# Convolution taps moved off VectorE in the first block, and the last block's last round done in two halves, in a float32 convolution and feed-forward kernel

## Chip, cores and metric

One core of one Trainium2 chip. The metric is the device time of one execution in microseconds; each run also has a profiled span, which begins and ends with the core's first and last recorded instruction and is about 1.8 us shorter. Spans are given to 0.1 us, so a difference with one is good to about 0.05 us. Ratios are the mean time of one kernel's fast runs over that of the other's of the same rounds, so not quite the ratio of the medians that I quote.

## The reference

```python
# x (8, 4096, 192), weight (8, 7), w_in (192, 2048), w_out (2048, 192)
w = softmax(weight)                          # 7 taps for each of 8 heads
c = causal 7-tap convolution of x along the sequence, taps by head
h = c.reshape(32768, 192) @ w_in
g = h * clip(h + 3, 0, 6) / 6
out = g @ w_out                              # float32
```

Of the kernel before, what the change touches and what calls it, by code (L numbers as in the profile page):

```python
# [8 lines left out]
ALU = mybir.AluOpType  # L9
# [7 lines left out]
def kernel(  # L17
# [21 lines left out]
    nc = tc.nc  # L39
# [3 lines left out]
    H, KC = weight.shape  # L43
# [3 lines left out]
    N = 512  # L47
# [107 lines left out]
    class Rounding:  # L155
# [10 lines left out]
        def load(self):  # L166
            self.st = self.load_words()
# [105 lines left out]
    def swap(part):  # L273

        to = slice(OTHER + part.start, OTHER + part.stop)
        nc.sync.dma_start(out=y[D2:P, to], in_=y[0:D2, part])  # L276
        nc.sync.dma_start(out=y[0:D2, to], in_=y[D2:P, part])
# [19 lines left out]
    def take():  # L297
        return free_banks.pop(0)

    def give(b):  # L300
        free_banks.append(b)
# [128 lines left out]
    def dff_half(k):  # L430
        return g[:, :, k // G, k % G]

    def mm(bank, j, x, w, q, ps_, first, last):

        cols = slice(q * QS, (q + 1) * QS)
        return [
            lambda p=p: nc.tensor.matmul(  # L437
                out=bank[j * QS : (j + 1) * QS], lhsT=w_out[:, p, w, cols], rhs=x[:, p],
                start=(first and p == ps_[0]), stop=(last and p == ps_[-1]),
                tile_position=(0, j * QS),  # L440
            )
            for p in ps_
        ]
# [5 lines left out]

    every = range(NP)  # L450

    def store_rows(i, k, q, xt, j, dma=nc.sync):

        t0 = i * TB + k * N
        dma.dma_start(
            out=out[t0 : t0 + N, q * QS : (q + 1) * QS].rearrange("(t r) d -> r t d", r=QS),
            in_=xt[j * QS : (j + 1) * QS].rearrange("r (t d) -> r t d", d=QS),
        )

    def out_direct(i, work):  # L460
# [41 lines left out]
        5: (None, T1), 6: (S2, T2), 7: (S3, T3),  # L502
    }

    def product(bank, j, n, q, ks=every):
        x, w = prod[n]
        return mm(bank, j, S1 if n == 5 else x, w, q, ks, True, True)

    def four(*parts):

# [5 lines left out]
    def three(n, n4, q4):  # L516
        return four(*[(n, q) for q in range(NQ)], (n4, q4))
# [11 lines left out]
    def rows(q):  # L529
        return slice(q * QS, (q + 1) * QS)  # L530
# [9 lines left out]
    def add(out, x, y, op=ALU.add):  # L540
        nc.vector.tensor_tensor(out=out, in0=x, in1=y, op=op)  # L541

    def store(i, c, k, half_, qs=range(NQ), queues=(nc.sync,)):

        xt = ot.tile([P, N], F32, name="xt")
        r = slice(qs[0] * QS, (qs[-1] + 1) * QS)
        nc.vector.transpose(out=xt[r], in_=c[r])  # L547
        for q in qs:
            store_rows(i, k, half_ * NQ + q, xt, q, queues[q % len(queues)])

    def sums_tiles():
        return (cs.tile([DH, N], F32, name=f"c{k}") for k in range(6))
# [3 lines left out]
    def out_last(i):  # L556

        both = nc.sync, nc.scalar
        p1, p2, p4, p5, u2, u3 = sums_tiles()
        b, bank = three(1, 2, 0)  # L560
        nc.scalar.copy(out=p1[:], in_=bank[m])
        piece(p2, 0, bank, NQ)
        give(b)
        g_sums(nc.vector, (2,), every, 4)
        b, bank = four((2, 1), (2, 2), (4, 0), (4, 1))
        for dst, q, j in ((p2, 1, 0), (p2, 2, 1), (p4, 0, 2), (p4, 1, 3)):
            piece(dst, q, bank, j)
        give(b)
        g_sums(nc.vector, (4,), every, 4)
        add(p2[:], p1[:], p2[:])  # L570
        store(i, p2, 0, 0)
        b7, bank7 = three(7, 5, 0)
        piece(p5, 0, bank7, NQ)
        b, bank = three(6, 5, 1)
        piece(p5, 1, bank, NQ)
        add(u2[:], p1[:], bank[m])
        give(b)
        add(u3[:], u2[:], bank7[m])
        give(b7)
        two = slice(0, 2 * QS)  # L580
        add(p4[two], u3[two], p4[two], ALU.subtract)
        store(i, p4, 1, 0, range(2))
        b, bank = by_quarters(5, 2)
        pieces(p5, 2, bank)
        give(b)
        add(u2[:], u2[:], p5[:])
        add(p5[:], u3[:], p5[:])
        store(i, p5, 1, 1)
        b, bank = three(3, 4, 2)
        add(u2[:], u2[:], bank[m])  # L590
        store(i, u2, 0, 1, queues=both)
        add(u3[rows(2)], u3[rows(2)], bank[rows(NQ)], ALU.subtract)
        store(i, u3, 1, 0, range(2, 3), queues=both[::-1])
        give(b)

    def out_strassen(i, conv):
        p1, p2, p4, p5, u2, u3 = sums_tiles()
# [55 lines left out]
    with tc.manual_schedule():  # L653
        nc.vector.tensor_reduce(out=sm[:], in_=e_sb[:], axis=AX.X, op=ALU.add)
        nc.vector.tensor_scalar_add(sm[:], sm[:], 1e-9)
        nc.vector.reciprocal(sm[:], sm[:])
        nc.vector.tensor_tensor(
            out=c_sb[:], in0=e_sb[:], in1=sm[:].to_broadcast([P, KC]), op=ALU.mult
        )

        thirds = [slice(s, s + 1) for s in range(K3)]
        pe_third = K3 - 1
        b = take()
        for _ in range(3):

            nc.tensor.matmul(
                out=psum[:, b], lhsT=zeros[:, 0:P], rhs=zeros[:], start=True, stop=True
            )
        for k in range(KC):
            nc.scalar.mul(diag[:, k], ident[:], c_sb[:, k : k + 1])  # L670
            nc.tensor.matmul(
                out=psum[:, b], lhsT=diag[:, k], rhs=x_tiles[0][:, pe_third, k : k + N],
                start=(k == 0), stop=(k == KC - 1),
            )
        conv0 = conv_units(0, thirds[:pe_third], 2)
        per = len(conv0) // pe_third
        for k, u in enumerate(conv0):
            if k == 5:
                split(0)
                clamp(0)  # L680
            elif k == per - 3:
                join(0, more=False)
            elif k == per:
                nc.scalar.copy(out=y[:, pe_third], in_=psum[:, b])
                give(b)
                swap(thirds[0])
                swap(thirds[pe_third])
                load(AHEAD)
                split(1)
                clamp(1)  # L690
            elif k == per + 6:
                split(2)
                join(1)
                clamp(2)
            u()
        swap(thirds[1])
        split(3)
        split(4)
        join(2)
        clamp(3)  # L700


        parts = [(c, group) for p in range(0, NP, 2) for group in (OWN, OTHER)
                 for c in (p, p + 1)]
        early = [(c, group, (take(), take())) for c, group in parts[:4]]
        order = (0, pe_third, 1)
        for c in range(2):
            for slot, group, bs in early:
                if slot == c:
                    for s in order[:2]:  # L710
                        h_mm(c, group, bs, s, order)
        for c, group, bs in early:
            h_mm(c, group, bs, order[2], order)

        slots = [0, 1, 2, 3, 5, 6, 8, 10, 12, 14]
        n = 3
        for slot, (c, group) in enumerate(parts):
            first = slot < len(early)
            if first:
                bs = early[slot][2]  # L720
            else:
                bs = take(), take()
                for s in range(K3):
                    h_mm(c, group, bs, s)
            more = slot in slots

            def between():
                if more:
                    join(n)
                    clamp(n + 1)  # L730

            if slot == 6:
                x_tiles[1] = load_x(1)
            h_out(c, group, bs, (lambda: None) if first else between)
            if more:
                split(n + 2)
                if first:
                    between()
                n += 1
        while n < len(units):  # L740
            join(n)
            clamp(n + 1)
            split(n + 2)
            n += 1
        w_sums()
        start_pools.close()
        ss = ctx.enter_context(tc.tile_pool(name="ss", bufs=1))
        p5s = ctx.enter_context(tc.tile_pool(name="p5s", bufs=3))
        cs = ctx.enter_context(tc.tile_pool(name="cs", bufs=1))
        ot = ctx.enter_context(tc.tile_pool(name="ot", bufs=4))  # L750

        def conv_and_swap(i):
            return conv_units(i, [slice(0, K3)]) + [lambda: swap(slice(0, K3)), y_sums]

        out_direct(0, conv_and_swap(1))
        x_tiles[2] = load_x(2)

        S1 = ss.tile([P, NP, N], F32, name="s1")[:]
        left = []
        for i in range(1, NB):  # L760
            h_phase(left)
            if i + 1 < NB:
                left = out_strassen(i, conv_units(i + 1, [slice(0, K3)]))
            else:
                out_last(i)
            if i + 2 < NB:
                x_tiles[i + 2] = load_x(i + 2)
# [33 lines left out]
```

## The kernel before: what the change touches

The kernel works through 32 blocks of 1024 tokens. The channels are in three thirds of 64; the tile `y` holds, for each third, 512 tokens in the lower and the other 512 in the upper 64 partitions ("own"). A swap by DMA gives each half the other's tokens ("other"). Both orders are multiplied with the 8 pairs of `w_in` units; a relu (ScalarE) and a gate (VectorE) turn each bank (the piece of TensorE's result memory, PSUM, that takes one product) into `g`; then `g` is multiplied with `w_out`. From block 1 on this is a Strassen scheme. The weights arrive as float64 words, and each of 16 units is rounded to float32 by `split` (VectorE), `clamp` (ScalarE) and `join` (VectorE, then a GpSimd product); `AHEAD` units are loaded in advance. A *pair* is, from here on, a pair of banks: 16 of them, counted from 0, make the first block's first projection (the multiplication with `w_in`), 12 matmul instructions each. In the code cuts `...` stands for what is left out.

The start, with VectorE making thirds 0 and 1 in halves of 256 tokens and TensorE making third 2 through diagonal matrices:

```python
        for k in range(KC):
            nc.scalar.mul(diag[:, k], ident[:], c_sb[:, k : k + 1])
            nc.tensor.matmul(out=psum[:, b], lhsT=diag[:, k], rhs=x_tiles[0][:, pe_third, k : k + N], ...)
        ...
        conv0 = conv_units(0, thirds[:pe_third], 2)      # 14 half taps for third 0, 14 for third 1
        for k, u in enumerate(conv0):
            if k == 5:         split(0); clamp(0)
            elif k == per - 3: join(0, more=False)
            elif k == per:
                nc.scalar.copy(out=y[:, pe_third], in_=psum[:, b]); give(b)
                swap(thirds[0]); swap(thirds[pe_third]); load(AHEAD)
                split(1); clamp(1)
            elif k == per + 6: split(2); join(1); clamp(2)
            u()
        swap(thirds[1])
        split(3); split(4); join(2); clamp(3)
        ...                                              # four pairs of banks are begun in thirds 0, 2, then third 1
        slots = [0, 1, 2, 3, 5, 6, 8, 10, 12, 14]        # bank pairs at which a unit is joined
```

The end of the last block:

```python
        b, bank = three(3, 4, 2)                         # the last 32 matmuls, 512 tokens wide
        add(u2[:], u2[:], bank[m])
        store(i, u2, 0, 1, queues=both)                  # transpose, then one DMA for 32 rows
        add(u3[rows(2)], u3[rows(2)], bank[rows(NQ)], ALU.subtract)
        store(i, u3, 1, 0, range(2, 3), queues=both[::-1])
```

## Time and profile before

| | before |
|---|---|
| time, median of 6 runs | 2410.84 us (2410.76 to 2410.96) |
| span | 2409.1 us |
| TensorE busy | 2399.2 us |
| first product (matmul with w_out) on the chain | 58.87 us |
| start of the last product phase | 2366.65 us |
| end of the last transpose | 2405.79 us |

TensorE is nearly the whole span. The *first product* is where the chain that ended last goes over from the first projection to the first multiplication with `w_out`; whatever the start wins must be won there. The *tail* is the time from the start of the last product phase to the end of the span, 42.45 us before. The four VectorE operations behind the last matmul (columns: start us, length us, engine, line, operation, operands, count, idle time before and what ended it):

```profile
2402.91 0.68 DVE L541 TENSOR_TENSOR c<-c,psum 96x512 f32<-96x512 f32 x1 [0.77 <-PE psum L437]
2403.63 0.71 DVE L547 STREAM_TRANSPOSE xt<-c 96x512 f32<-96x512 f32 x1
2404.37 0.69 DVE L541 TENSOR_TENSOR c<-c,psum 32x512 f32<-32x512 f32 x1
2405.09 0.70 DVE L547 STREAM_TRANSPOSE xt<-c 32x512 f32<-32x512 f32 x1
```

VectorE idles 0.77 us until the whole round is multiplied, then works 2.9 us; that idle time is what the change of the last round aims at.

### The profile page before, as it was taken

The page shows a single profiled execution, that of the slowest core. Times are in us where ns is not written, and L with a number is a line of the kernel's source. Part 1 is how long each engine was busy: PE and PEld are TensorE (multiplying, and loading weights), DVE is VectorE, ACT ScalarE, POOL GpSimd, SP SyncE. Part 2 cuts the span into 40 slices and gives each one's busy share as a digit, 9 for nine tenths or more (in the row PEclk, how much of TensorE's full clock was granted, in tenths as well). Part 3 has the DMA queues.
Part 4 walks back from the last instruction along what each step waited for, and adds up shares of the span by engine and source line. Part 5 has one row for each costly group of instructions (what it writes and reads, how often), then busy time and mean ns, then how long its engine had stood idle before and what let it go on. Part 6 is the DMA issues. An engine that isn't in the chain of part 4 may idle for free.

```text
span 2409.1 us, 40076 instructions
## 1 busy us (share of the span) xinstructions
PE 2399.2 (100%) x16468; PEld 1008.8 (42%) x16468; DVE 2088.8 (87%) x2534; ACT 1077.1 (45%) x1827; POOL 671.3 (28%) x280
## 2 busy tenths in 40 slices
PE   9999999999999999999999999999999999999998
PEld 4334444334444344443444434444334444344443
DVE  8788888988888888898888898888898888888896
ACT  7234553345543355433454334553335543355433
POOL 2423321233221333122332223322233312333122
PEclk9999999999999999999999999999999999999999
DMA  5211122101122011221112211122201122111210
GB/s 145 40 26 29 27 40 40 39 18 26 39 41 40 19 35 27 40 41 22 32 27 40 41 34 21 27 40 40 40 18 34 30 40 40 21 34 27 40 27 14
DMA packets 227336, 84.65 MB, mean 35 GB/s; under 512 B 205456, under 2 KB 210576, under 8 KB 227152
## 3 DMA queue, kind: packets, MB, share of 16 engines
q1 hardware_dynamic: 225848, 81.56, 17.1%
q8 instruction: 129, 2.11, 0.4%
q10 hardware_dynamic: 1208, 0.27, 0.1%
q14 instruction: 55, 0.45, 0.1%
q0 software_dynamic: 96, 0.26, 0.0%
HBM read 31.72 MB, written 25.17 MB: 24 GB/s over the span
## 4 chain that ended last, share of the span: by engine, by line
PE 99%; DVE 1%; DMA 0%; issue 0%; ACTq 0%; SPq 0%; DVEq 0%
PE psum L311 50%; PE psum L437 48%; DVE y L263 0%; DMA x<-in_x_dram 0%; DMA y<-y 0%; DVE c L541 0%; ACTq L92 0%; DVE scale L174 0%; DVE y L259 0%; DVE sig L199 0%; DVE scale L195 0%; DVE top L178 0%; DVE xt L547 0%; SPq L276 0%; DVEq L259 0%
## 5 line engine op out<-in xcount | busy, mean ns | idle before, releaser
L437 PE MATMUL psum<-g,w_out 128*32 128x512 f32 x9312 | 1163.6, 592 | 0.0
L311 PE MATMUL psum<-y,w_in 64*128 64x512 f32 x3664 | 885.1, 592 | 2.1 <-DVE y L263 1.9
L497 POOL TENSOR_TENSOR s<-g 128x1024 f32<-128x1024 f32 x124 | 293.5, 2367 | 1645.1 <-DVE g L321 1645.1
L317 ACT ACTIVATE r<-psum,half 128x512 f32<-128x512 f32 x1024 | 641.3, 688 | 241.3 <-PE psum L311 234.2
L437 PEld LDWEIGHTS psum<-g,w_out 128*32 128x32 f32 x9312 | 337.4, 110 | 811.7 <-issue 769.9
L321 DVE SCALAR_TENSOR_TENSOR g<-r,psum 128x512 f32<-128x512 f32 x1024 | 641.8, 681 | 4.8 <-ACT r L317 1.1
L437 PE MATMUL psum<-s,w_out 128*32 128x512 f32 x1488 | 638.5, 592 | 0.0
L311 PEld LDWEIGHTS psum<-y,w_in 64*128 64x128 f32 x3664 | 430.2, 187 | 378.7 <-issue 299.4
L311 PE MATMUL psum<-y,w_in_t 64*128 64x512 f32 x1984 | 523.8, 592 | 0.0
L403 DVE TENSOR_TENSOR psum<-psum,p 128x512 f32<-128x512 f32 x496 | 324.6, 694 | 196.0 <-PE psum L311 187.3
L263 DVE SCALAR_TENSOR_TENSOR y<-x,c_sb,y 128x1536 f32<-128x1536 f32 (+1 forms) x210 | 416.6, 1991 | 6.6
L533 ACT COPY c<-psum 32x512 f32<-32x512 f32 x188 | 108.7, 578 | 600.7 <-PE psum L437 599.9
L497 POOL TENSOR_TENSOR g<-g 128x1024 f32<-128x1024 f32 x124 | 338.0, 2725 | 9.7
L311 PEld LDWEIGHTS psum<-y,w_in_t 64*128 64x128 f32 x1984 | 247.1, 186 | 194.3 <-issue 124.9
L541 DVE TENSOR_TENSOR c<-c,psum 32x512 f32<-32x512 f32 (+1 forms) x187 | 128.1, 685 | 81.8 <-ACT c L533 75.8
L396 ACT COPY psum<-psum 128x512 f32<-128x512 f32 x248 | 138.9, 571 | 72.6 <-PE psum L311 57.4
L437 PEld LDWEIGHTS psum<-s,w_out 128*32 128x32 f32 x1488 | 162.4, 110 | 1.2 <-issue 1.2
L399 ACT COPY p<-psum 128x512 f32<-128x512 f32 x248 | 133.2, 591 | 40.7 <-PE psum L311 40.0
L497 DVE TENSOR_TENSOR g<-s,g 128x2048 f32<-128x2048 f32 x62 | 139.3, 2287 | 3.9 <-POOL g L497 2.3
L497 DVE TENSOR_TENSOR g<-g 128x2048 f32<-128x2048 f32 x62 | 139.4, 2289 | 2.0 <-PE psum L437 1.0
L601 ACT COPY c<-psum 96x512 f32<-96x512 f32 x30 | 17.4, 581 | 174.5 <-PE psum L437 174.5
L606 ACT COPY c<-psum 96x512 f32<-96x512 f32 x30 | 17.4, 581 | 170.0 <-PE psum L437 170.0
(46 smaller groups left out, 431.9 us busy)
## 6 DMA issues: line engine op xcount, KB each, us to landing
out_dram<-xt SPq DMA_DIRECT2D x382, 64.0 KB, 2.0
y<-y SPq DMA_DIRECT2D x62, 384.0 KB, 4.8
x<-in_x_dram SPq DMA_DIRECT2D x55, 388.5 KB, 5.7
stage<-in_moe_w_in_dram SPq DMA_DIRECT2D x16, 192.0 KB, 4.4
stage<-in_moe_w_out_dram SPq DMA_DIRECT2D x8, 384.0 KB, 5.2
x<-in_x_dram SPq DMA_DIRECT2D x7, 384.0 KB
y<-y SPq DMA_DIRECT2D x6, 128.0 KB, 2.3
x<-in_x_dram SPq DMA_DIRECT2D x2, 128.0 KB, 4.4
```

The lines of the kernel that those rows point to most:

```text
L263: nc.vector.scalar_tensor_tensor(out=to, in0=x[:, part, k + t : k + t + W], scalar=c, in1=to, op0=ALU.mult, op1=ALU.add,)
L311: nc.tensor.matmul(out=psum[:, b], lhsT=w[r], rhs=y[r, third_of_y], start=start, stop=stop, skip_group_check=onto,)
L317: nc.scalar.activation(r6, h, ACT.Relu, bias=half[:], scale=1.0 / 6.0)
L321: nc.vector.scalar_tensor_tensor(out=out, in0=r6, scalar=1.0, in1=h, op0=ALU.min, op1=ALU.mult)
L396: nc.scalar.copy(out=psum[:, bank["b"]], in_=psum[:, bank["a"]])
L399: nc.scalar.copy(out=self.p5[:], in_=psum[:, bank["e"]])
L403: nc.vector.tensor_tensor(out=psum[:, to], in0=psum[:, bank["b"]], in1=self.p5[:], op=ALU.add)
L437: lambda p=p: nc.tensor.matmul(out=bank[j * QS : (j + 1) * QS], lhsT=w_out[:, p, w, cols], rhs=x[:, p], start=(first and p == ps_[0]), sto ...
L497: engine.tensor_tensor(out=o[:, r], in0=a[:, r], in1=b[:, r], op=op)
L533: nc.scalar.copy(out=dst[rows(q)], in_=src[rows(j)])
L541: nc.vector.tensor_tensor(out=out, in0=x, in1=y, op=op)
L601: nc.scalar.copy(out=p1[:], in_=bank[m])
```

## The change

The intent at the start: take work off VectorE (tap 0 of third 1 to ScalarE, taps 5 and 6 to TensorE), exchange TensorE's own third 2 as soon as it is copied, and spread the joins so that the first pairs are less crowded. Some lines only change place: split 3, and with it clamp 3, now comes behind join 2. At the end: do the last round in two halves of 256 tokens, so that VectorE begins while TensorE still multiplies.

```diff
+        pe_taps = KC - 2
+        def pe_tap(b, part, k, first): nc.tensor.matmul(...)     # one tap through a diagonal matrix
         for k in range(KC):
             nc.scalar.mul(diag[:, k], ident[:], c_sb[:, k : k + 1])
+            pe_tap(b, pe_third, k, 0)
+        nc.scalar.mul(y[:, 1], x0[:, 1, 0:N], c_sb[:, 0:1])      # tap 0 of third 1
+        b1 = take()
+        pe_tap(b1, 1, pe_taps, pe_taps)                          # tap 5
+        order = (pe_third, 0, 1)
...
-        for k, u in enumerate(conv0):
+        for k, u in enumerate(conv0[: per + 2 * pe_taps]):
             elif k == per - 3:
                 join(0, more=False)
+                split(1)
                 nc.scalar.copy(out=y[:, pe_third], in_=psum[:, b])
                 swap(thirds[pe_third])
                 clamp(1)
             elif k in (per, per + 1):
+                if k == per:
+                    swap(thirds[0]); load(AHEAD)
+                    begin(0, OWN)                                # first pair, thirds 2 and 0
+                    pe_tap(b1, 1, pe_taps + 1, pe_taps)          # tap 6
+                continue
+            elif k == per + 4: join(1); split(2); clamp(2)
+        add(y[:, 1], psum[:, b1], y[:, 1]); give(b1)
         swap(thirds[1])
-        split(3); split(4); join(2); clamp(3)
+        join(2); split(3); clamp(3); split(4)
...
-        slots = [0, 1, 2, 3, 5, 6, 8, 10, 12, 14]
+        slots = [0, 1, 3, 4, 6, 7, 9, 10, 12, 13]
... (last round of the last block)
+        for t in range(0, N, N // 2):
+            b = take(); bank = psum[:, b]; ts = slice(t, t + N // 2)
+            side_by_side(...)                                    # the same products, tokens ts
+            add(u2[:, ts], u2[:, ts], bank[m, ts])
+            store(i, u2, 0, 1, queues=both, tokens=ts)
+            add(u3[rows(2), ts], u3[rows(2), ts], bank[rows(NQ), ts], ALU.subtract)
+            store(i, u3, 1, 0, range(2, 3), queues=both[::-1], tokens=ts)
+            give(b)
```

More of the change, by code (lines that the diff above doesn't have):

```diff
@@ L431, in dff_half, with mm @@
         return g[:, :, k // G, k % G]
-    def mm(bank, j, x, w, q, ps_, first, last):
+    def mm(bank, j, x, w, q, ps_, first, last, tokens=slice(0, N)):
         cols = slice(q * QS, (q + 1) * QS)
@@ L437, in mm @@
             lambda p=p: nc.tensor.matmul(
-                out=bank[j * QS : (j + 1) * QS], lhsT=w_out[:, p, w, cols], rhs=x[:, p],
+                out=bank[j * QS : (j + 1) * QS, tokens], lhsT=w_out[:, p, w, cols],
+                rhs=x[:, p, tokens],
                 start=(first and p == ps_[0]), stop=(last and p == ps_[-1]),
@@ L450, with store_rows @@
     every = range(NP)
-    def store_rows(i, k, q, xt, j, dma=nc.sync):
+    def store_rows(i, k, q, xt, j, dma=nc.sync, tokens=slice(0, N)):
         t0 = i * TB + k * N
         dma.dma_start(
-            out=out[t0 : t0 + N, q * QS : (q + 1) * QS].rearrange("(t r) d -> r t d", r=QS),
-            in_=xt[j * QS : (j + 1) * QS].rearrange("r (t d) -> r t d", d=QS),
+            out=out[t0 + tokens.start : t0 + tokens.stop, q * QS : (q + 1) * QS].rearrange("(t r) d -> r t d", r=QS),
+            in_=xt[j * QS : (j + 1) * QS, tokens].rearrange("r (t d) -> r t d", d=QS),
         )
@@ L503, with product @@
     }
-    def product(bank, j, n, q, ks=every):
+    def product(bank, j, n, q, ks=every, **tokens):
         x, w = prod[n]
-        return mm(bank, j, S1 if n == 5 else x, w, q, ks, True, True)
+        return mm(bank, j, S1 if n == 5 else x, w, q, ks, True, True, **tokens)
     def four(*parts):
@@ L541, in add, with store @@
         nc.vector.tensor_tensor(out=out, in0=x, in1=y, op=op)
-    def store(i, c, k, half_, qs=range(NQ), queues=(nc.sync,)):
+    def store(i, c, k, half_, qs=range(NQ), queues=(nc.sync,), tokens=slice(0, N)):
         xt = ot.tile([P, N], F32, name="xt")
         r = slice(qs[0] * QS, (qs[-1] + 1) * QS)
-        nc.vector.transpose(out=xt[r], in_=c[r])
+        nc.vector.transpose(out=xt[r, tokens], in_=c[r, tokens])
         for q in qs:
-            store_rows(i, k, half_ * NQ + q, xt, q, queues[q % len(queues)])
+            store_rows(i, k, half_ * NQ + q, xt, q, queues[q % len(queues)], tokens)
     def sums_tiles():
@@ L588, in out_last @@
         store(i, p5, 1, 1)
-        b, bank = three(3, 4, 2)
-        add(u2[:], u2[:], bank[m])
-        store(i, u2, 0, 1, queues=both)
-        add(u3[rows(2)], u3[rows(2)], bank[rows(NQ)], ALU.subtract)
-        store(i, u3, 1, 0, range(2, 3), queues=both[::-1])
-        give(b)
+        for t in range(0, N, N // 2):
+            b = take()
+            bank = psum[:, b]
+            ts = slice(t, t + N // 2)
+            side_by_side(*[
+                product(bank, j, n, q, tokens=ts)
+                for j, (n, q) in enumerate([(3, 0), (3, 1), (3, 2), (4, 2)])
+            ])
+            add(u2[:, ts], u2[:, ts], bank[m, ts])
[3 more added lines that the diff above has]
+            give(b)
     def out_strassen(i, conv):
@@ L662, with pe_tap @@
         pe_third = K3 - 1
+        pe_taps = KC - 2
+        x0 = x_tiles[0]
+        def pe_tap(b, part, k, first):
+            nc.tensor.matmul(
+                out=psum[:, b], lhsT=diag[:, k], rhs=x0[:, part, k : k + N],
+                start=(k == first), stop=(k == KC - 1),
+            )
         b = take()
@@ L670, with begin @@
             nc.scalar.mul(diag[:, k], ident[:], c_sb[:, k : k + 1])
-            nc.tensor.matmul(
-                out=psum[:, b], lhsT=diag[:, k], rhs=x_tiles[0][:, pe_third, k : k + N],
-                start=(k == 0), stop=(k == KC - 1),
-            )
+            pe_tap(b, pe_third, k, 0)
[3 more added lines that the diff above has]
+        order = (pe_third, 0, 1)
+        parts = [(c, group) for p in range(0, NP, 2) for group in (OWN, OTHER)
+                 for c in (p, p + 1)]
+        early = {}
+        def begin(c, group):
+            early[c, group] = take(), take()
+            for s in order[:2]:
+                h_mm(c, group, early[c, group], s, order)
         conv0 = conv_units(0, thirds[:pe_third], 2)
         per = len(conv0) // pe_third
-        for k, u in enumerate(conv0):
+        for k, u in enumerate(conv0[: per + 2 * pe_taps]):
             if k == 5:
@@ L682 @@
                 join(0, more=False)
-            elif k == per:
+                split(1)
                 nc.scalar.copy(out=y[:, pe_third], in_=psum[:, b])
                 give(b)
-                swap(thirds[0])
                 swap(thirds[pe_third])
-                load(AHEAD)
-                split(1)
                 clamp(1)
-            elif k == per + 6:
+            elif k in (per, per + 1):
+                if k == per:
+                    swap(thirds[0])
+                    load(AHEAD)
+                    begin(0, OWN)
+                    pe_tap(b1, 1, pe_taps + 1, pe_taps)
+                continue
+            elif k == per + 4:
+                join(1)
                 split(2)
-                join(1)
                 clamp(2)
             u()
+        add(y[:, 1], psum[:, b1], y[:, 1])
+        give(b1)
         swap(thirds[1])
+        join(2)
         split(3)
+        clamp(3)
         split(4)
-        join(2)
-        clamp(3)
-        parts = [(c, group) for p in range(0, NP, 2) for group in (OWN, OTHER)
-                 for c in (p, p + 1)]
-        early = [(c, group, (take(), take())) for c, group in parts[:4]]
-        order = (0, pe_third, 1)
-        for c in range(2):
-            for slot, group, bs in early:
-                if slot == c:
-                    for s in order[:2]:
-                        h_mm(c, group, bs, s, order)
-        for c, group, bs in early:
-            h_mm(c, group, bs, order[2], order)
-        slots = [0, 1, 2, 3, 5, 6, 8, 10, 12, 14]
+        for c, group in ((0, OTHER), (1, OWN), (1, OTHER)):
+            begin(c, group)
+        for c, group in parts[: len(early)]:
+            h_mm(c, group, early[c, group], order[2], order)
+        slots = [0, 1, 3, 4, 6, 7, 9, 10, 12, 13]
         n = 3
@@ L719 @@
             if first:
-                bs = early[slot][2]
+                bs = early[c, group]
             else:
```

## The prediction

> **What bounds the kernel now.** I read the page first, then the chain that ended last in order of time, then the timelines of each engine in the first 60 us and the last 15 us, and last the busy time by one-microsecond windows of the start.
>
> The page says that this kernel is a dense TensorE stream with a thin beginning and a thin end:
>
> ```profile
> PE 2399.2 (100%) x16468; PEld 1008.8 (42%) x16468; DVE 2088.8 (87%) x2534; ACT 1077.1 (45%) x1827; POOL 671.3 (28%) x280
> PE 99%; DVE 1%; DMA 0%; issue 0%; ACTq 0%; SPq 0%; DVEq 0%
> ```
>
> So only what is not TensorE on the chain can be won by a change of order. The chain, in order of time, shows both places:
>
> ```profile
> 18.37 3.19 DVE y L263 x7
> ...
> 21.81 0.47 DVE y L263
> 22.28 0.28 DVE scale L174
> 22.57 0.25 SPq L276
> 22.81 0.04 issue
> 22.86 2.40 DMA y<-y
> 25.25 0.04 issue
> 25.30 33.57 PE psum L311 x152
> 58.87 41.34 PE psum L437 x384
> ```
>
> From 6.67 us the chain is VectorE: taps of the convolution and the splits and joins of the first weight units. It makes the last third of y, y goes through the exchange of halves (22.3 to 25.25), and at 25.30 TensorE starts a run that never waits for long again until 2402.9. Everything after 25.30 shifts with it. The end is four VectorE operations and a store after the last matmul: add, transpose, subtract, transpose, from 2402.91 to 2405.79, and the span closes at 2409.1. The part that a reordering can touch is thus the delay before 25.30, about 1 us of waits in the first 35 us after it, and about 6 us of tail: at most some 10 us of 2410.8, and 2% would be 48 us.
>
> VectorE at the start has no gaps worth naming, which is why tap work given to another engine counts (columns: start us, length us, instruction):
>
> ```profile
> 11.30 0.55 DVE L195 SCALAR_TENSOR_TENSOR scale<-stage,scale 128x384 uint32<-128x384 uint32 x1
> 11.77 0.55 DVE L199 SCALAR_TENSOR_TENSOR sig<-top,sig 128x384 f32<-128x384 uint32 x1
> 12.24 2.01 DVE L263 SCALAR_TENSOR_TENSOR y<-x,c_sb,y 128x256 f32<-128x256 f32 x3
> 14.17 0.35 DVE L174 TENSOR_SCALAR scale<-stage 128x384 uint32<-128x384 uint32 x1
> ```
>
> A half tap (128x256) costs 0.395 us start to start (six of them lie between 8.92 and 11.30), a first tap (tensor_scalar) 0.27, a split 0.535 (two starts, 14.17 to 14.71), a join 0.94 (11.30 to 12.24). Three taps from 12.24 to 14.17 should have taken 1.19 us and took 1.93: 0.75 us lost while GpSimd multiplied w_in (12.40 to 13.57). The same happens once more after the second join, at 18.69.
>
> The ScalarE timeline shows what paces the first gates:
>
> ```profile
> 22.59 0.62 ACT L186 ACTIVATE sig<-scale,bias_e 128x384 f32<-128x384 uint32 x1 [3.54 <-DVE scale L174]
> 23.24 0.61 ACT L189 ACTIVATE scale<-sig,bias_e 128x384 uint32<-128x384 f32 x1
> 23.88 0.56 ACT L192 ACTIVATE sig<-stage 128x384 f32<-128x384 uint32 x1
> 24.35 1.25 ACT L317 ACTIVATE r<-psum,half 128x512 f32<-128x512 f32 x2
> ```
>
> The relu of the first pair waits behind the clamp of weight unit 3 (22.59 to 24.35). With a clamp per pair the relus come every 2.90 us (24.35, 27.25, 30.16, 33.07), while TensorE needs 12 instructions x 0.2145 = 2.57 us per pair (a warm start-to-start of 0.43 for two). Banks come free with the gates, some 1.9 us after the relu starts.
>
> **What the Trainium skill says.** SBUF — State Buffer, section "Who interferes with whom": a VectorE instruction with two SBUF inputs, or in a 2-port mode, and a GpSimd instruction that reads SBUF lock each other out. The trace agrees: a tap of 0.47 us took 1.22 at 12.63, beside the GpSimd product. TensorE: Matmul & The Clock Gate, Part 1: an idle TensorE falls to half clock after a window of about 3.4 us. The trace agrees: granted clock 0.50 in 16 to 18 us, after TensorE idled from 12.5 to 14.4. VectorE: DVE Perf Modes, section on the errata: a float32 tensor_tensor takes (N+151)/0.96 ns; 512 columns give 691 and the trace has 684 to 694; so I estimate 424 ns for 256. DMA: Bandwidth & Descriptors, "Anatomy of one DMA": about 2 us fixed, the rest by bytes; a 64 KB store lands here after 2.0 to 2.2 us, so half the bytes should save little.
>
> **The change, step by step.**
>
> 1. VectorE up to y's third 1. Removed: two first-tap halves (0.53 us), now one ScalarE multiply, and four halves of taps 5 and 6 (1.58), now TensorE. Added: one 128x512 addition of the bank (0.65). Net saving 1.46. The two lock collisions stay, since both joins stay ahead. Against it: the ScalarE multiply is queued ahead of clamp 0 and must wait for that third of x (issued 4.27, 5.1 us to land: 9.37), so clamp 0 begins at about 10.1, not 8.77, and join 0 waits some 0.25 us. So third 1 is done near 22.28 - 1.46 + 0.25 = 21.07, and its exchange lands 2.95 us later, near 24.0 instead of 25.25.
>
> 2. TensorE up to there. Its own third (2) is now exchanged as soon as ScalarE has copied it (13.1, landing near 16). Work from the first weight unit (ready near 13.85, because join 0 is later): 40 projection instructions x 0.2145 = 8.58, plus one tap of two instructions at 0.43 = 0.86; the other tap fits before. Split 1 now comes before the last taps of third 0, so that third is ready near 15.05, 0.8 later than before (14.25): TensorE waits there 0.35 us, and perhaps 0.3 for its exchange (15.05 + 2.95 = 18.0). 13.85 + 9.44 + 0.65 = 23.95. TensorE is then just in time for the exchange at 24.0; before, it had about 0.9 us in hand. The idle time before it is short, so I take the clock to stay up.
>
> 3. The first pairs. The 152 instructions start near 24.05 instead of 25.30. But clamp 3 now follows join 2 and split 3: 21.07 + 0.94 + 0.35 gives 22.4, against 22.59, so the first relu is at 24.2, hardly 0.2 earlier. The gates free banks at 26.07, 28.98, 31.88; TensorE could begin pairs 4, 5, 6 at 25.77, 28.64, 31.55: it waits about 0.3 us three times. With joins at pairs 0, 1, 3, 4 the third pair has no clamp, so relu 3 comes at 31.1 instead of 33.07, and from pair 7 there is no wait. Last projection ends near 34.45 + 9 x 2.57 = 57.6; by the same sum the kernel before ends at 58.46, having waited at pairs 7 and 8 only (0.24 and 0.32). Gain of the start: 0.85 us. Later joins have room: weight unit 13, needed about 8.6 us into the second product, was ready at 63.2 of 67.4.
>
> 4. The last round. Matmuls of 256 columns, twice as many: 2 x 16 groups x 0.215 = 6.87 us, as before; the doubled weight loads (0.13 per group of four) hide under 0.215. The first half is ready 3.4 us before the end, but VectorE is busy with the earlier results until 2402.14. Then eight half operations instead of four: additions 0.42, transposes 0.44 (0.71 less 256/0.96 ns), plus 0.03 each: 3.6 us, ending near 2405.75 against 2405.79. What is won is the 0.77 us that VectorE idled; what is paid is four more fixed costs of about 0.17. The last store has 32 KB, not 64: at the 133 GB/s that the last windows show, 0.25 us less. Gain 0.3.
>
> Sum: 2410.8 - 0.85 - 0.3 = 2409.65. I say 2409.6.
>
> **The rivals.** (a) The whole 1.25 us of step 1 arrives at the end, because the relus and clamps overlap better than I count: the chain shows ScalarE nowhere before, which speaks for it; the 2.90 us spacing speaks against. About 2409.2, or 2408.7 if the split also dodges one lock. (b) The wait moves: the ScalarE multiply delays clamp 0 more than I think, or TensorE, now without slack, meets a half clock as in 16 to 18 us, which doubled the time of some 3 us of work. Then start gain is zero or negative: 2410.5 to 2411.2. For it: all three engines are nearly full from 12 to 24. Against: less TensorE idling. (c) The tail: the fourth-last transpose buffer. The split makes seven transposed tiles over four buffers, so the last transpose must wait for the store of three tiles before, issued 2403.06 and landed near 2405.1, just when it is wanted (2405.25). If that store is slow, the tail gains nothing: +0.3. Conversely, if half operations are cheaper, the tail gains up to 0.7.
>
> **Range and chances.** Runs of one kernel differ by under 0.1 us, so the range is my error alone: best cases of (a) and (c) together give 2408.2, (b) with no tail gain 2411. I take 2408.2 to 2410.9. No reading of this profile finds 48 us either way: within 2% is nearly certain.
>
> **What would show it.** Right: third 1's addition ends near 21, the exchange lands near 24, projections end near 57.6, first relu near 24.2 with short waits on gates at pairs 4 to 6; VectorE unbroken from 2401.3 to the last transpose, and a last store of half the bytes. Wrong: clock 0.50 within 15 to 24 us, VectorE waiting for ScalarE at join 0 by over 0.5 us, gates not the thing TensorE waits for, or 256-column matmul groups slower than 0.215 us.

## The result and the profile after

| | before | after |
|---|---|---|
| time, median of 6 | 2410.84 us | 2410.26 us (2409.86 to 2411.30) |
| ratio of the fast runs, 95% interval | 1 | 0.9998 (0.9986 to 1.0011) |
| spans of the 6 runs after | 2409.1 (the profiled run) | 2408.5, 2408.5, 2408.5, 2408.4, 2408.1, 2408.5 |
| first product on the chain | 58.87 us | 58.50 us |
| tail (last product phase to end of span) | 42.45 us | 42.07 us |

The gain is 0.6 us where I said 1.2. The median lies within the predicted range of 2408.2 to 2410.9, but so does the time of the kernel before, so this alone shows little; one of the six runs (2411.30) lies outside of it. The page is unchanged in kind. On the chain the long run of TensorE begins 8 us earlier than before:

```profile
PE 2400.5 (100%) x16536; PEld 1019.8 (42%) x16536; DVE 2089.4 (87%) x2533; ACT 1078.4 (45%) x1828; POOL 672.2 (28%) x280
```

```profile
17.22 41.28 PE psum L311 x184
58.50 41.34 PE psum L437 x384
```

So 184 projection instructions took 41.28 us, while 184 x 0.2145 (the warm pitch) is 39.5. Some 1.8 us of waits are inside by that sum. The timelines of VectorE and ScalarE at the places that the prediction named:

```profile
20.48 0.69 DVE L542 TENSOR_TENSOR y<-psum,y 128x512 f32<-128x512 f32 x1
...
34.56 0.55 DVE L195 SCALAR_TENSOR_TENSOR scale<-stage,scale 128x384 uint32<-128x384 uint32 x1
35.03 1.35 DVE L199 SCALAR_TENSOR_TENSOR sig<-top,sig 128x384 f32<-128x384 uint32 x1
36.31 1.27 DVE L321 SCALAR_TENSOR_TENSOR g<-r,psum 128x512 f32<-128x512 f32 x2
```

```profile
24.18 1.25 ACT L317 ACTIVATE r<-psum,half 128x512 f32<-128x512 f32 x2
```

Third 1 is done at 21.17 (predicted 21.07), the first relu is at 24.18 (24.2). But the second operation of a join took 1.35 us in place of 0.55. GpSimd was at the product of the join before it:

```profile
34.72 1.25 POOL L203 TENSOR_TENSOR w_in<-sig,scale 128x384 f32<-128x384 f32 x1 [3.09 <-DVE sig L199]
```

The joins of pairs 3 and 4 follow each other directly: the first comes behind pair 3's gates, the second ahead of pair 4's gates. The second is held by the first's GpSimd product, and pair 4's gates come late, at 36.31. TensorE's weight loads show who waited:

```profile
37.63 2.44 PEld L311 LDWEIGHTS psum<-y,w_in 64*128 64x128 f32 x13 [0.24 <-DVE g L321]
```

In the tail, VectorE begins at 2401.94 with no idle time, as intended, but stops ahead of its last operation:

```profile
2404.72 0.42 DVE L542 TENSOR_TENSOR c<-c,psum 32x256 f32<-32x256 f32 x1
2405.57 0.44 DVE L548 STREAM_TRANSPOSE xt<-c 32x256 f32<-32x256 f32 x1 [0.43 <-DMA out_dram<-xt]
```

The block's seventh transposed tile waits for a store that still reads its buffer. The chain names the store:

```profile
2403.79 1.68 DMA out_dram<-xt
```

It is the one of the tile two before (transposed at 2403.33), which landed at 2405.47. The last store of the kernel, in both cases one for 32 rows, has half the bytes (first line before, second after; columns: count, size, us from issue to landing):

```profile
out_dram<-xt ACTq DMA_DIRECT2D x1, 64.0 KB, 1.8
out_dram<-xt ACTq DMA_DIRECT2D x1, 32.0 KB, 1.5
```

**Theory, before the experiments.** The start loses what it wins to the first pairs: to the lock between VectorE and GpSimd at the joins of pairs 3 and 4, and to the clamp of unit 3 that now stands behind a join. The tail is shorter by 0.8 us behind the last transpose, which I put down to the smaller last store, and loses 0.4 to the four buffers. **Rivals.** The start brings nothing and the tail all; or the exchange and TensorE's own work, not gates and clamps, set the first projection.

### The profile page after: what moved, and what is told of

The parts are those of the page before. It is cut to its first block, busy times and chain, and to the rows that moved or that the text cites. A ratio compares the mean times of both kernels' runs of the same rounds, so it can differ in the third digit from the quotient of the medians.

```text
span 2408.5 us, 40221 instructions
## 1 busy us (share of the span) xinstructions
PE 2400.5 (100%) x16536; PEld 1019.8 (42%) x16536; DVE 2089.4 (87%) x2533; ACT 1078.4 (45%) x1828; POOL 672.2 (28%) x280
## 4 chain that ended last, share of the span: by engine, by line
PE 99%; DVE 1%; DMA 0%; issue 0%; ACTq 0%; ACT 0%; DVEq 0%
PE psum L311 51%; PE psum L437 48%; DVE c L542 0%; DMA x<-in_x_dram 0%; DVE y L263 0%; DMA out_dram<-xt 0%; DVE xt L548 0%; DVE top L178 0%; ACTq L92 0%; PE psum L676 0%; DVE scale L174 0%; DVE y L259 0%; ACT c L534 0%; DVE scale L195 0%; DVEq L548 0%
## 5 line engine op out<-in xcount | busy, mean ns | idle before, releaser
L437 PE MATMUL psum<-g,w_out 128*32 128x512 f32 (+1 forms) x9376 | 1163.7, 590 | 0.0
L311 PEld LDWEIGHTS psum<-y,w_in 64*128 64x128 f32 x3664 | 437.1, 187 | 369.6 <-issue 290.6
L542 DVE TENSOR_TENSOR c<-c,psum 32x512 f32<-32x512 f32 (+2 forms) x189 | 128.4, 679 | 81.2 <-ACT c L534 75.9
L399 ACT COPY p<-psum 128x512 f32<-128x512 f32 x248 | 133.2, 590 | 40.4 <-PE psum L311 39.5
```

The source lines that it names most:

```text
L311: nc.tensor.matmul(out=psum[:, b], lhsT=w[r], rhs=y[r, third_of_y], start=start, stop=stop, skip_group_check=onto,)
L399: nc.scalar.copy(out=self.p5[:], in_=psum[:, bank["e"]])
L437: lambda p=p: nc.tensor.matmul(out=bank[j * QS : (j + 1) * QS, tokens], lhsT=w_out[:, p, w, cols], rhs=x[:, p, tokens], start=(first and p ...
L542: nc.vector.tensor_tensor(out=out, in0=x, in1=y, op=op)
```

## The experiments

All outputs are right. The kernel before, on three chips, had medians of 2410.92, 2410.89 and 2410.82 us. Every 95% interval of the ratio includes 1 (for e8_best 0.9980 to 1.0005). What is said below of tenths of a microsecond rests on the small scatter and on the one trace that each kernel has.

| run | change against | time, median us (range) | span, median us | first product |
|---|---|---|---|---|
| e1_start_only | after, last round as before | 2410.81 (2410.77 to 2410.91) | 2409.0 | 58.55 |
| e2_tail_only | after, start as before | 2410.53 (2410.48 to 2410.66) | 2408.8 | 59.00 |
| e3_slots_before | after, joins as before | 2410.24 (2410.16 to 2410.61) | 2408.5 | 58.68 |
| e4_slots_apart | after, joins of pairs 3, 4 apart | 2410.07 (2410.04 to 2411.30) | 2408.3 | 58.22 |
| e5_buf5 | after, five buffers | 2409.79 (2409.38 to 2410.10) | 2408.0 | 58.10 |
| e6_clamp_early | after, clamp 3 ahead of join 2 | 2409.72 (2409.65 to 2409.75) | 2408.0 | 57.89 |
| e7_no_taps | after, taps 5, 6 on VectorE | 2411.23 (2410.58 to 2411.32) | 2409.5 | 59.37 |
| e8_best | after, with e4, e5 and e6 | 2409.03 (2408.97 to 2409.09) | 2407.2 | 57.47 |
| e9_three_taps | e8, taps 4, 5, 6 on TensorE | 2408.90 (2408.84 to 2409.76) | 2407.1 | 57.43 |
| e10_own_third_second | after, third 2 exchanged second | 2411.81 (2411.68 to 2413.03) | 2410.0 | 59.91 |

In most of these kernels spans differ less than times do (not in e7, e9 and e10, whose five spans range over 0.7, 0.9 and 1.4 us), so mechanisms are read from spans and traces.

### e1_start_only and e2_tail_only: which part is worth what

The edit of e1 puts back the five lines of the last round; that of e2 puts back the start and the old list of joins.

> The start of the change with the last round of the kernel before. My theory (the start is worth what its trace showed at the first product: its first L437 matmul at 58.50 instead of 58.87 us, so 0.37 us; the tail is worth another 0.2 to 0.4 us of span): span near 2408.7, time 0.3 to 0.4 us under before, and the four last VectorE operations as before (0.70 us each). Rival (the start is worth all of the span's 0.6 us and the split of the last round nothing): span 2408.5. If the wide scatter of the changed kernel (1.4 us over six runs, 0.2 before) comes from the start, it stays here; if from the tail, runs agree within 0.2 us.

> The start of the kernel before with the last round by halves. My theory: TensorE as before to the last matmul, then span 0.2 to 0.4 us shorter (2408.8), the last transpose waiting some 0.4 us for the store of the tile three before (four buffers). Rival (tail worth nothing, start all): span 2409.1. Theory for the scatter: with eight small stores on two queues at the end, the time outside of the span varies, so the scatter of about 1 us is here and not in the run with the start alone.

The start alone won 0.11 us of time and the tail alone 0.39. For the start I had expected 0.3 to 0.4. In e1 the first product is 0.32 us earlier than before and the last product phase only 0.12 (2366.53 against 2366.65): some of the gain is given back in mid-run. The chain shows where. In each trace one or two projection phases of 38.08 us take 0.2 to 0.35 more: one in the trace before (at 1956.89), two in e1 and in the changed kernel (at 174 and 1734). In the changed kernel:

```profile
174.12 38.43 PE psum L311 x174
212.55 36.19 PE psum L437 x336
248.74 38.08 PE psum L311 x174
```

The two phases agree until, 31 us into each, a VectorE addition begins 0.35 us later in the first, though ScalarE and TensorE had delivered at the same times. No transfer was under way then. Its cause stays open.

The tail of e2 is 42.12 us, as in the changed kernel (42.07), against 42.45 before. Its last transpose waited 0.48 us, and its span was 2408.8, as expected. The theory for the scatter fell: neither run alone scatters.

### e4_slots_apart: the lock at pairs 3 and 4

```diff
-        slots = [0, 1, 3, 4, 6, 7, 9, 10, 12, 13]
+        slots = [0, 1, 3, 5, 6, 8, 9, 11, 12, 14]
```

> The changed kernel with the joins at pairs 0, 1, 3, 5, 6, 8, 9, 11, 12, 14, so that the joins of pairs 3 and 4 no longer follow each other. My theory (the predicted 0.85 us of the start became 0.37 because two joins back to back on VectorE at 33.6 to 36.3 us, the second held 0.8 us by the GpSimd product of the first, put the gates of pair 4 at 36.31 instead of 35.5, and TensorE waited for that bank until 37.63): the gates of pair 4 at about 34.7, no wait of TensorE after pair 6, first product at 57.9 to 58.1, span 0.4 to 0.6 us under the changed kernel. Rival (TensorE loses that time elsewhere, or the wait moves to a later join): first product unchanged at 58.5.

The chain, and VectorE where the joins had met:

```profile
17.39 40.83 PE psum L311 x184
58.22 41.34 PE psum L437 x384
```

```profile
34.27 0.55 DVE L199 SCALAR_TENSOR_TENSOR sig<-top,sig 128x384 f32<-128x384 uint32 x1
34.93 1.29 DVE L321 SCALAR_TENSOR_TENSOR g<-r,psum 128x512 f32<-128x512 f32 x2
```

Pair 4's gates begin at 34.93 instead of 36.31, and TensorE waits for no gate after pair 6. The same 184 instructions take 40.83 us in place of 41.28, so the collision cost 0.45. (This execution entered its projection 0.17 us later, which is why the first product is 58.22 and not 58.05.) Of the span only 0.2 us was seen: in the trace the first product is 0.28 us earlier, and two of the mid-run delays (38.43 and 38.41 us, together 0.2 us more than those of the changed kernel) take most of that back. The theory of the lock holds; the expected 0.4 to 0.6 us of span did not come.

### e5_buf5: the wait in the tail

```diff
-        ot = ctx.enter_context(tc.tile_pool(name="ot", bufs=4))
+        ot = ctx.enter_context(tc.tile_pool(name="ot", bufs=5))
```

> The changed kernel with five transpose buffers in place of four. My theory (the last transpose waits 0.43 us for the store that still reads its buffer): the last transpose starts at about 2405.15 instead of 2405.57 and the span is 0.3 to 0.4 us shorter, 2408.1. Rival (the end is set by the stores' own queue, not by the buffer): transpose earlier, span unchanged. If the scatter comes from this wait, it falls to 0.2 us.

The wait is gone:

```profile
2404.49 0.44 DVE L548 STREAM_TRANSPOSE xt<-c 32x256 f32<-32x256 f32 x1
```

But the tail is 41.86 us, only 0.2 shorter than the changed kernel's 42.07: from the end of the last transpose to the end of the span it is now 2.67 us, and it was 2.49 with the wait. So half of the 0.43 was lost again behind the last transpose (in e8, with the same buffers, the tail is 41.95). Most of the rest of this run's gain is not the buffer's. In the profiled execution the joins of pairs 3 and 4, though still adjacent, did not collide: the second operation, at 35.09, took 0.58 us, and it was GpSimd that waited. First product at 58.10, 184 instructions in 40.83 us, as in e4; so it is the collision that costs 0.45 us, and not where e4 put the later joins. Of the six traces in which these joins are adjacent, VectorE was held in five (the changed kernel, e1, e6, e7 and e10, 1.35 to 1.36 us each) and GpSimd in this one. In the five, GpSimd's product began 0.16 to 0.17 us after the VectorE operation ahead of the held one, here 0.19. Some hundredths of a microsecond thus seem to decide which engine gets the lock; this is inferred from six traces. The spans of 2407.6 in the profiled run and 2407.9 to 2408.2 in the others fit that, as does the one short span of the changed kernel (2408.1 among 2408.5); it is not shown, since only one execution of each has a trace.

### e3_slots_before: what the spread is worth

```diff
-        slots = [0, 1, 3, 4, 6, 7, 9, 10, 12, 13]
+        slots = [0, 1, 2, 3, 5, 6, 8, 10, 12, 14]
```

> The changed kernel with the joins at the pairs of the kernel before (0, 1, 2, 3, 5, 6, 8, 10, 12, 14): undoes the spread alone. My theory (a clamp at each of the first four pairs keeps the relus 2.90 us apart, so the gates of pairs 3 and 4 come at about 34.8 and 37.7 and TensorE waits for banks at pairs 7 and 8): first product at 58.3 to 58.6, so as the changed kernel in the runs where its back-to-back joins collide (58.50), and 0.4 us later than where they don't (58.1); span 2408.4 to 2408.7. Rival (the spread is what pays at the start): first product at 58.9 or later, span 2409 or more.

First product at 58.68, time 2410.24 us. As the changed kernel collides at pairs 3 and 4, its spread is worth 0.18 us at the first product and nothing in the time. With the old list TensorE waits for gates at pairs 7 and 8, as the prediction's sum had it for the kernel before. The theory's window of 58.3 to 58.6 was missed by 0.08; the rival's (58.9 or later) was not reached.

### e6_clamp_early: the clamp in front of the first relu

```diff
         swap(thirds[1])
-        join(2)
         split(3)
         clamp(3)
+        join(2)
         split(4)
```

> The changed kernel with split 3 and clamp 3 ahead of join 2 (two lines moved), so that VectorE and ScalarE have the clamp out of the way 0.94 us earlier. My theory (the relus behind clamp 3, not the exchange or TensorE's start, set when banks come free for pairs 4 to 6): first relu at about 23.2 instead of 24.18, the waits of TensorE on gates between 28 and 33 us gone, first product at 57.4 to 57.8 instead of 58.5, span 0.7 to 1.0 us shorter. Rival (the exchange of the last third, landing near 24.0, and TensorE's own work set it): relu earlier, first product unchanged at 58.1 to 58.5.

```profile
23.50 1.32 ACT L317 ACTIVATE r<-psum,half 128x512 f32<-128x512 f32 x2
```

```profile
17.25 40.64 PE psum L311 x184
57.89 41.34 PE psum L437 x384
```

The first relu came 0.68 us earlier, the waits on gates at pairs 5 and 6 vanished, and the first product is 0.6 us earlier, with a span 0.5 us shorter. The mechanism is right and the size a little less than expected (57.4 to 57.8, and 0.7 to 1.0 us of span). Two things remain: the relu was then held by TensorE's own work (clamp 3 was done by 23.5), and pairs 3 and 4 still collide, with a second join operation of 1.36 us.

### e7_no_taps and e10_own_third_second: undoing the other parts of the start

```diff
-        pe_taps = KC - 2
+        pe_taps = KC              # and the two pe_tap calls, the addition and its bank removed
```

> The changed kernel with taps 5 and 6 of third 1 back on VectorE (tap 0 stays on ScalarE, the rest of the order stays). My theory (VectorE's order up to third 1 sets the exchange and, through join 2 and split 3, the clamp and relus): third 1 ready 0.9 us later (22.1), first relu at 25.1 instead of 24.18, first product 0.7 to 1.0 us later, 59.2 to 59.5, so slower than the kernel before (58.87), span 2409.2 to 2409.5. Rival (the taps on TensorE bring nothing because TensorE was the bound from 15 us and gets 0.86 us of work back): first product at 58.5 or earlier.

```profile
25.03 34.34 PE psum L311 x152
59.37 41.34 PE psum L437 x384
```

Third 1 was done at 22.06 instead of 21.17, TensorE waited for its exchange until 25.03, as in the kernel before, and the first product came 0.87 us later. So the taps carry the whole gain: without them the rest of the new order is 0.5 us *worse* than the kernel before (59.37 against 58.87). What tap 0 on ScalarE and the earlier place of split 1 are worth was not tested: they stay in every run with the new start.

```diff
             elif k == per - 3:
                 ...
-                swap(thirds[pe_third])
             elif k == per:
                 swap(thirds[0])
+                swap(thirds[pe_third])
```

> The changed kernel with third 2 exchanged behind third 0 as before, so that its exchange lands near 18.7 to 19.0 instead of 16. My theory (in the changed kernel the gates of pairs 2 to 4 set the end of the first projection, so TensorE's earlier work has slack): TensorE waits 1.2 to 1.8 us at 17 and reaches the last exchange late, at about 25.3, but the waits on gates vanish in return: first product within 0.3 us of 58.50, span 2408.4 to 2408.8. Rival (TensorE was just in time, so the delay goes through): first product at 59.7 to 60.0, span 2409.7.

```profile
19.26 40.65 PE psum L311 x183
59.91 41.34 PE psum L437 x384
```

Here my theory fell and the rival was right: TensorE waited at 17 us until 19.26, about 2.0 us, and 1.41 us of that arrived at the first product. What I had left out: the first pair's own projection is behind that wait too, so the first relu moved to 25.57, and the gates with it. Only the other 0.6 us was taken up by shorter waits later on, so TensorE before 24 us has little slack in the changed kernel. Exchanging its own third first is needed there. That the kernel before could do without it because its third 1 came later is argued, not tested.

### e8_best and e9_three_taps: the repairs together

> Three repairs together: joins of pairs 3 and 4 apart, five transpose buffers, split 3 and clamp 3 ahead of join 2. If my theory of each holds they add up, being in different places: first product at 57.1 to 57.5, no wait in the tail, span 2406.6 to 2407.3, time 2408.4 to 2409.1. Rival (they overlap, since all three only move the same wait): span no better than with five buffers alone, 2407.6 to 2408.2.

```profile
17.16 40.31 PE psum L311 x184
57.47 41.34 PE psum L437 x384
```

First product 57.47, span 2407.2 us, time 2409.03 us, with all five runs within 0.12 us. That is 1.86 us under the kernel before and about 1.2 under the changed kernel. The repairs of start and tail add up. TensorE waits for no gate any more in the first projection. Then the next question: is VectorE's third 1 still the limit?

```diff
-        pe_taps = KC - 2
+        pe_taps = KC - 3          # one more pe_tap ahead of the first weight unit
```

> The repaired kernel (joins apart, five buffers, clamp 3 early; first product at 57.47 us on its chain, span 2407.2) with three taps of third 1 on TensorE, two of them in its idle time before the first weight unit. My theory (TensorE is now the bound from 15 us: its instructions run without a wait from 17 to 24 but for 0.4 us at third 0's exchange and 0.34 us at the addition of third 1): VectorE finishes third 1 at about 20.3 instead of 21.1, but only the 0.34 us is won: first product at 57.0 to 57.3, span 2406.8 to 2407.1. Rival (VectorE's third 1 is still what sets the start): 0.8 us won, first product at 56.7, span 2406.4.

VectorE finished third 1 at 20.48 instead of 21.10, and the first product stayed (57.43). The chain of this run is TensorE from 6.25 us on. That is what the theory said of TensorE, but even the 0.34 us wait was hardly won (57.0 to 57.3 expected): GpSimd had the first weight unit ready at 13.68 us, and TensorE, still at its own taps, came to it only at 14.17 (13.57 in e8). Two of the five times are 0.8 us longer than the others, so I would keep e8.

## Why the prediction was right, and where it was not

1. **Third 1.** Right: 21.17 for 21.07. The wait for ScalarE at join 0 was 0.11 us, not 0.25.
2. **TensorE just in time at 24.** Right, and shown twice: in the trace no wait for the last exchange, and in e10, where a delay ahead of it goes through. First weight unit at 13.63 (13.85), third 0 at 15.04 (15.05), waits of 0.27 and 0.41 us for 0.35 and 0.3. The granted clock was 1.00 in every microsecond window from 10 to 27, where it had been 0.50 in 16 to 18: rival (b) did not come.
3. **First pairs.** Right in the mechanism: first relu at 24.18, clamp 3 behind join 2 as the brake (e6). Wrong in one step, "from pair 7 there is no wait". I summed join costs without asking what stands next to what: the new list puts two joins back to back, the first's GpSimd product holds the second, pair 4's gates come at 36.31, and TensorE waits until 37.63 for pair 8. That cost 0.45 us (e4, and the trace of e5), so the gain of 0.85 became 0.37. Taking the collision away restores it: e4's 40.83 us put the first product at 58.05, 0.82 before the old 58.87.
4. **The tail.** The sum was near (0.3 predicted, 0.39 in e2), but by luck: two terms that were not in it cancelled. I had VectorE end 0.04 us early; in relation to the last product phase it ended 0.44 us later (39.58 against 39.14 us), since it waited 0.43 us for a buffer. Rival (c) had named such a wait, but for another store: the tile that it meant (transposed at 2401.20) had its last store issued at 2402.83 and landed at 2405.11, just in time. The store that was waited for is that of the tile two before, from 2403.79 to 2405.47. On the other side, the smaller last store saved what I had allowed, 0.3 us against 0.25 (1.5 us to landing in place of 1.8, issued at 2406.04 and 2405.83). But from the end of the last transpose to the end of the span it is 2.49 us in place of 3.31. The other 0.5 us lies behind the last landing, where the kernel before takes about 1.5 us to end and the changed one 0.9. I had not counted that, and its cause is not shown. My guess that half the bytes should save little was right for the landing alone.
5. **What was in no step.** Of the start's 0.3 to 0.4 us only 0.11 reached the time in e1, the difference going to VectorE delays of 0.2 to 0.35 us in mid-run. The kernel before has one too, so I should have allowed for a moving number of them. I also took the scatter of a kernel's times to be under 0.1 us and the range to be my error alone; the six times of the changed kernel range over 1.4 us.

Rival (a) was not seen: the relus did not overlap better than counted.

Left open: the cause of the mid-run delays; and the scatter of the changed kernel's times. It is mostly outside of the span: time less span is 1.72 to 1.85 us in most runs, 1.9 to 2.1 in seven (of e3, e4, e5, e8, e9 and e10), but 2.4 and 2.8 in two of the changed kernel, 2.90 in one of e4 and 2.89 in one of e9. Neither half of the change alone shows it, and neither do e6 and e7, which have both halves. Some spans stand out too, without a trace: 2408.8 in e7 (2409.3 to 2409.5 in the others), 2411.3 in e10 (2409.9 to 2410.0), 2407.7 in e9 (2406.8 to 2407.1).

## What to carry to other kernels

When one engine nearly fills the span, a reordering can win only its waits at the ends: list those first, with their sizes, and follow each of them through *every* engine that releases a buffer to it. Work moved off an engine pays only as far as the next releaser allows, here the clamp and the gates, so the order of two short instructions there (e6) was worth more at the first product (0.61 us) than the larger change (0.37). And splitting the last round for overlap multiplies tiles: count them against the buffers, look which store the last ones wait for, and count adjacent operations that share a lock.

## What the Trainium skill lacked or had wrong

- SBUF — State Buffer, "Who interferes with whom": the page says that issue order decides who blocks. Five traces agree (1.35 to 1.36 us for a VectorE operation of 0.55 us, behind a GpSimd product that had begun before it). In e5's trace the product had begun first too (34.81 against 35.09), and yet it was the product that was held (1.72 us in place of 1.0). The page does not say how such a row of requests, which differs between these traces by 0.02 to 0.03 us, is settled.
- TensorE: Matmul & The Clock Gate, Part 1: the page has the clock fall after an idle window of about 3.4 us. In the kernel before it was 0.50 for about 3.4 us (0.71 on average from 15 to 16 us, 0.50 from 16 to 18, 0.58 from 18 to 19) after TensorE had idled for only 1.9 us (12.49 to 14.39).
- DMA: Bandwidth & Descriptors: the fit in "Anatomy of one DMA" (a fixed cost plus bytes) is one for DMAs issued from GpSimd, and no section gives the time by size for small stores from the SyncE and ScalarE queues, as here. The median landing, with 128-byte rows, was 2.0 us for 64 KB and 1.7 to 1.8 for 32 KB; for the kernel's last store it was 1.8 and 1.5.
- VectorE: DVE Perf Modes, errata section: the estimate of 424 ns that its formula gives for a float32 addition of 256 columns holds (0.42 us measured). No page gives the time of the 32x32-block transpose at these sizes: 0.71 us for 512 columns, 0.44 for 256.
- No page has the single VectorE operations that begin 0.35 us late with their inputs ready, nor the time of up to 1.1 us that some executions take beyond the usual 1.8 us outside of their span.
